# Attention and feed-forward on one core: the first feed-forward unit of a turn is issued ahead of the scores of the last key group

## The chip, the cores and the metric

The kernel runs on one core of a Trainium2 chip. The metric is the device time of one execution, in microseconds (us); lower is better. PE is TensorE (matmuls; PEld its weight loads), DVE is VectorE, ACT is ScalarE, POOL is GpSimd, and SP is SyncE, whose queue issues most transfers.

## The reference

Cosine attention for 8 batches of 12 heads (448 tokens, head size 64), then a feed-forward layer on the joined heads:

```python
q_n = q / (np.linalg.norm(q, axis=-1, keepdims=True) + 1e-06)
k_n = k / (np.linalg.norm(k, axis=-1, keepdims=True) + 1e-06)
scores = np.matmul(q_n, k_n.transpose(0, 1, 3, 2)) / tau
attn = np.exp(scores - np.max(scores, axis=-1, keepdims=True))
attn = attn / (np.sum(attn, axis=-1, keepdims=True) + 1e-09)
x = np.matmul(attn, v)          # heads joined: 3584 x 768
h = x @ w_in                    # 768 x 2048
g = h * np.clip(h + 3.0, 0.0, 6.0) / 6.0
out = g @ w_out                 # 2048 x 768
```

## The kernel before, in words

The work is cut into 48 pairs of heads (6 pairs to a batch), numbered i. For a pair, normalised q and k are held transposed with the head size on the partitions. The keys of a pair fall into four groups (`GROUPS`, line 364): groups 0 to 2 are 128 keys of each of the two heads (two matmuls each), and group 3, "M", is the last 64 keys of both heads together (one matmul). The steps of a pair are functions, each called by a short name through `do` (line 653):

- `SC`, `scores` (line 367): the score matmuls of one group, one PSUM bank for each matmul (L394). Groups 0 to 2 read `kz`, group 3 reads `km` from pair 14 on.
- `EX`, `exps` (line 400): exp on ACT from each bank to `at` (L412), which frees the bank.
- `VA`, `values` (line 425): 8 matmuls of a group that accumulate attn times v into the PSUM tile `PV` (L434).
- `FI`, `finish_values` (line 445): reciprocal and product on DVE, giving `on` (L454, L455).
- `XB` and `XP` (lines 482 and 493): a DMA on SP that transposes `on` of one pair or of two pairs into `xT` (L486, L498), the input of the feed-forward layer.

The keys and queries ahead are prepared by `LQ` (load, L174, on SP), `SQ` (square on POOL, L203), `RE` (reduce on DVE, L215), `NO` (four short activations on ACT, L231 to L234), `NM` (normalise on POOL, L246), `XD` (a transposing DMA on SP into `tT`, L302), `CK` (copy of keys from `tT` to `kz` on DVE, L341) and `CS` (copy of the last group's keys from `tT` to `km` on POOL, L351, once for two pairs, in odd turns). `LV` loads v and `VC` casts it on POOL (L186, L265).

The feed-forward layer is a stream of units. A first-layer unit (`mm1_unit`, line 508) is 6 matmuls into one bank (L514), then a relu on ACT (L523) and a product on DVE (L529), which writes `gT`. A second-layer unit (`mm2_unit`, line 541) is 16 matmuls of 384 columns (L550), a copy on ACT or DVE in turn (L561, L563), and two stores on SP (L571). A batch's first-layer units need `xT` of its six pairs. `whole_units(n)` (`UU`, line 639) issues n units, each with its work on ACT, DVE and SP.

Scores of groups and units of both kinds take PSUM banks from one ring of six (`next_bank`, line 136; `ring`, line 630), always the next one. A bank is taken again only when its reader has read it: the exp for scores, relu and product for a first-layer unit, the copy for a second-layer unit.

The schedule is written out by hand: every engine runs its instructions in the order in which the program issues them, and semaphores are put in between where one step needs another. Pairs 0 to 17 follow a list (`PLAN`). From pair 18 on (`FIRST`, line 18) each pair is one turn of the loop at line 700. In such a turn the program issues the last value step of the pair before that is still due for group 3, the scores of groups 0 to 2 (six matmuls, which take six banks in a row), their six exps, the value steps of groups 1 and 2 of the pair before, `FI` of that pair, and then the stretch that the change touches: group 3's scores and exp, the transposes on SP, one unit, the preparation of later pairs, and the remaining units (three or four a turn in all). The turn ends with the value step of group 0 of its own pair. After pair 47 the rest of the stream follows.

Of the kernel before, what the change touches and what calls it, by code (L numbers as in the profile page):

```python
# [61 lines left out]
def kernel(  # L62
# [590 lines left out]
    def do(op, *args):  # L653
        OPS[op](*args)
        key = (op,) + tuple(a for a in args if isinstance(a, int))
        if op not in ("RE", "NM", "LQ"):
            issued.add(key[:3] if op == "SC" else key)
# [27 lines left out]
    SC = [psum_s.tile([128, 2, 512], FP32, name=f"SC{n}", tag=f"SC{n}") for n in range(2)]  # L685
# [14 lines left out]
    for i in range(FIRST, NP):  # L700
        n_u = len(units[i])
        even = i % 2 == 0

        def prepare(*what):
            for op, n, *args in what:
                if n < (NP // 2 if op in ("NO", "LV") else NP):
                    do(op, n, *args)

        if i > FIRST:
            do("VA", i - 1, 3)  # L710
        for g in range(3):
            do("SC", i, g)
        for g in range(3):
            do("EX", i, g)
        for g in range(1, 4):
            if ("VA", i - 1, g) not in issued:
                do("VA", i - 1, g)
        do("FI", i - 1)
        do("SC", i, 3)
        do("EX", i, 3)  # L720

        if (i - 1) % HP > 3:
            do("XB", i - 1)
        elif even:
            do("XP", i - 2)
        if even:
            prepare(("XD", i + 2))
        do("UU", 1)
        if not even:
            prepare(("CS", i + 1))  # L730
        prepare(("SQ", i + 5, "p", 0, 7))
        n = 2
        do("UU", n - 1)
        if not even:
            prepare(("CK", i + 1), ("CK", i + 2))
        if not even:
            prepare(("NO", (i + 3) // 2))
        do("UU", n_u - n)
        prepare(("NM", i + 3, "p"), ("VC", i + 2, "p"), ("RE", i + 5))
        if even:  # L740
            prepare(("XD", i + 3))
        prepare(("LQ", i + 7))
        if not even:
            prepare(("LV", (i + 5) // 2))
        do("VA", i, 0)
# [42 lines left out]
```

## Time and profile before

| | us |
|---|---|
| median of three runs | 421.07 |
| lowest and highest of them | 419.57, 422.46 |
| the profiled execution, its time | 420.79 |
| the profiled execution, its span | 418.7 |

The span runs from the first to the last instruction on the engines; the 2.1 us beside it lie around the program. In the profile, L514 and the like are lines of the kernel; a tile's buffer number is left out, so the four banks M0 to M3 of the ring are all "M", and the other two are "Y" and "Z". The length of a matmul in the timeline (0.35 us for 448 columns) overlaps with that of the next, which starts before it ends; the spacing of the starts shows how fast PE goes. A square bracket behind a row gives the idle time of its engine before it and what ended it.

The loop's first turn, 18, begins on PE at 114.97 us; turn 19 at 124.65, turn 22 at 149.33, and the last, 47, at 347.90. A turn takes 6.75 to 9.7 us. The granted clock of TensorE was 1.00.

### The profile page before, as it was taken

The page shows a single profiled execution, that of the slowest core. Times are in us where ns is not written, and L with a number is a line of the kernel's source. Part 1 is how long each engine was busy: PE and PEld are TensorE (multiplying, and loading weights), DVE is VectorE, ACT ScalarE, POOL GpSimd, SP SyncE. Part 2 cuts the span into 40 slices and gives each one's busy share as a digit, 9 for nine tenths or more (in the row PEclk, how much of TensorE's full clock was granted, in tenths as well). Part 3 has the DMA queues.
Part 4 walks back from the last instruction along what each step waited for, and adds up shares of the span by engine and source line. Part 5 has one row for each costly group of instructions (what it writes and reads, how often), then busy time and mean ns, then how long its engine had stood idle before and what let it go on. Part 6 is the DMA issues. An engine that isn't in the chain of part 4 may idle for free.

```text
span 418.7 us, 9613 instructions
## 1 busy us (share of the span) xinstructions
PE 411.0 (98%) x3792; PEld 242.1 (58%) x3792; DVE 214.5 (51%) x419; ACT 268.3 (64%) x591; POOL 183.8 (44%) x190
## 2 busy tenths in 40 slices
PE   7999999999999999999999999999999999999996
PEld 5666556556655555555555555555555555655564
DVE  6898677855445445465445453555454343315410
ACT  6899998885557755857756775776765674105400
POOL 7899646454235466355375365374372300000000
PEclk9999999999999999999999999999999999999999
DMA  8999999789797866767986958777865431330033
GB/s 292 298 245 253 179 279 229 152 138 205 163 182 193 187 168 152 175 176 139 183 196 126 201 136 181 177 155 154 182 165 76 87 66 34 69 77 20 2 75 75
DMA packets 91564, 65.31 MB, mean 156 GB/s; under 512 B 56064, under 2 KB 89984, under 8 KB 91520
## 3 DMA queue, kind: packets, MB, share of 16 engines
q1 hardware_dynamic: 87728, 58.37, 61.2%
q0 software_dynamic: 3712, 6.29, 8.7%
q8 instruction: 29, 0.48, 0.5%
q14 instruction: 15, 0.12, 0.1%
q10 hardware_dynamic: 80, 0.05, 0.1%
HBM read 47.19 MB, written 11.01 MB: 139 GB/s over the span
## 4 chain that ended last, share of the span: by engine, by line
PE 97%; DVE 1%; DMA 1%; issue 0%; ACT 0%; ACTq 0%
PE M L514 24%; PE M L550 23%; PE PV L434 12%; PE Z L550 7%; PE Y L514 6%; PE Y L550 6%; PE Z L514 6%; PE M L394 5%; PE PV L621 3%; PE Y L394 1%; PE Z L394 1%; PE SC L394 1%; DMA xT<-on 1%; PE Z L291 1%; PE Y L616 1%; PE SC L391 0%
## 5 line engine op out<-in xcount | busy, mean ns | idle before, releaser
L550 PEld LDWEIGHTS <-gT 128*128 128x128 bf16 x912 | 88.6, 98 | 58.4
L412 ACT ACTIVATE at<-M 128x448 bf16<-128x448 f32 x199 | 96.8, 565 | 33.4 <-PE M L394 21.1
L514 PEld LDWEIGHTS <-w_in_sb 128*128 128x128 bf16 x768 | 73.3, 97 | 68.7 <-issue 8.2
L514 PE MATMUL M<-xT,w_in_sb 128*128 128x448 bf16 x522 | 107.2, 352 | 0.8 <-DMA xT<-on 0.8
L550 PE MATMUL M<-w_out_sb,gT 128*128 128x384 bf16 (+1 forms) x592 | 99.3, 324 | 0.0
L246 POOL TENSOR_TENSOR nrm<-raw,r 128x896 bf16<-128x896 f32 (+1 forms) x48 | 77.8, 1626 | 38.3 <-ACT r L234 28.6
L529 DVE SCALAR_TENSOR_TENSOR gT<-u,M 128x448 bf16<-128x448 bf16 x87 | 52.8, 619 | 56.5 <-ACT u L523 56.3
L203 POOL TENSOR_TENSOR sq<-raw 128x896 f32<-128x896 f32 (+3 forms) x39 | 63.5, 1629 | 13.3 <-DMA raw<-in_q_dram 6.3
L434 PEld LDWEIGHTS <-at 128*128 128x128 bf16 (+1 forms) x1536 | 54.8, 97 | 24.6 <-issue 15.4
L523 ACT ACTIVATE u<-M,bias 128x448 bf16<-128x448 f32 x87 | 55.3, 659 | 15.6 <-PE M L514 15.5
L434 PE MATMUL PV<-vx,at 128*128 128x65 bf16 (+1 forms) x1536 | 64.3, 194 | 0.2 <-DVE on L455 0.2
L215 DVE TENSOR_REDUCE n<-sq 128x14 f32<-128x896 f32 (+1 forms) x50 | 51.8, 1041 | 5.9 <-ACT sq L201 5.7
L351 POOL COPY km<-tT 64x128 bf16<-64x128 bf16 x34 | 9.9, 292 | 97.8 <-DMA tT<-nrm 65.2
L412 ACT ACTIVATE at<-Z 128x448 bf16<-128x448 f32 x48 | 27.0, 563 | 12.3 <-PE M L394 12.2
L455 DVE TENSOR_TENSOR on<-PV,rc 128x512 bf16<-128x512 f32 x48 | 33.2, 692 | 1.7
L563 DVE COPY o<-M 128x384 f32<-128x384 f32 x18 | 10.0, 558 | 46.6 <-PE M L550 38.6
L561 ACT COPY o<-M 128x384 f32<-128x384 f32 (+1 forms) x19 | 8.9, 471 | 38.5 <-PE M L550 37.6
L394 PE MATMUL M<-tT,kz 64*128 64x448 bf16 (+1 forms) x175 | 31.3, 351 | 0.0
L550 PE MATMUL Z<-w_out_sb,gT 128*128 128x384 bf16 (+1 forms) x176 | 29.1, 319 | 0.0
L265 POOL CAST vx<-vr 128x512 bf16<-128x512 f32 x44 | 27.6, 630 | 1.3 <-DMA vr<-in_v_dram 1.2
L412 ACT ACTIVATE at<-Y 128x448 bf16<-128x448 f32 x47 | 26.6, 567 | 2.2 <-PE Z L394 2.2
L514 PE MATMUL Y<-xT,w_in_sb 128*128 128x448 bf16 x126 | 27.3, 352 | 0.0
(78 smaller groups left out, 336.8 us busy)
## 6 DMA issues: line engine op xcount, KB each, us to landing
vr<-in_v_dram SPq DMA_DIRECT2D x96, 128.0 KB, 4.1
raw<-in_k_dram SPq DMA_DIRECT2D x24, 448.0 KB, 4.4
raw<-in_q_dram SPq DMA_DIRECT2D x24, 448.0 KB, 4.1
out_dram<-o SPq DMA_DIRECT2D x110, 96.0 KB, 2.2
w_in_sb<-in_moe_w_in_dram POOLq DMA_DIRECT2D x4, 768.0 KB, 11.1
w_out_sb<-in_moe_w_out_dram POOLq DMA_DIRECT2D x4, 768.0 KB, 9.3
tT<-nrm SPq DMA_TRANSPOSE x34, 3.4
xT<-on SPq DMA_TRANSPOSE x25, 4.0
```

The costliest lines, as they stand in the source:

```text
L203: engines[e].tensor_tensor(out=o, in0=i, in1=i, op=ALU.mult)
L215: nc.vector.tensor_reduce(out=n2s[d % 2][:, j % 2, c], in_=sq[:, :, :, :].rearrange("p g c d -> p (g c) d")[:, c, :], axis=AX.X, op=ALU.add,)
L246: engines[e].tensor_tensor(out=nrm[:, :, g, :].rearrange("p c g d -> p g c d"), in0=raw_of[j][:, g, :, :], in1=rs[d % 2][3][:, j % 2, :] . ...
L265: (engines[e].copy if e == "a" else engines[e].tensor_copy)(out=o, in_=f)
L394: nc.tensor.matmul(o, ks, qt[rows], start=True, stop=True)
L412: nc.scalar.activation(out=o, in_=x, func=AF.Exp, scale=inv_tau)
L434: nc.tensor.matmul(pv_out(j, h), at[rows, n, q_cols(i // HP, j)], vt[rows, 3 + h if name == "M" else 5 * h + int(name[1]), :], start=(name ...
L455: nc.vector.tensor_tensor(out=on[:, :, :, :].rearrange("p j h d -> p h j d"), in0=pv4[:, :, :, 0:D], in1=rc[:, :, :].to_broadcast([128, 2, ...
L514: nc.tensor.matmul(ps[:, 0:S], w_in_sb[:, cc, fc * 128 : (fc + 1) * 128], x[:, cc, 0:S], start=(cc == 0), stop=(cc == CC - 1),)
L523: nc.scalar.activation(out=u[:, :], in_=ps[:, 0:S], func=AF.Relu, bias=half_bias, scale=1.0 / 6.0)
L529: nc.vector.scalar_tensor_tensor(out=g[:, fc, c0 : c0 + S], in0=u[:, :], scalar=1.0, in1=ps[:, 0:S], op0=ALU.min, op1=ALU.mult,)
L550: nc.tensor.matmul(ps[:, 0:width], lhs, w_out_sb[:, fc, cols], start=(fc == 0), stop=(fc == FCN - 1),)
```

## The change

Group 3's scores and its exp are issued behind the turn's first unit, and so behind the transposes on SP that stand ahead of that unit, in turns 18 to 47. Nothing else is altered.

```diff
             if ("VA", i - 1, g) not in issued:
                 do("VA", i - 1, g)
         do("FI", i - 1)
-        do("SC", i, 3)
-        do("EX", i, 3)
 
         if (i - 1) % HP > 3:
             do("XB", i - 1)
...
         if even:
             prepare(("XD", i + 2))
         do("UU", 1)
+        do("SC", i, 3)
+        do("EX", i, 3)
         if not even:
             prepare(("CS", i + 1))
         prepare(("SQ", i + 5, "p", 0, 7))
```

As banks are handed out in the order of issue, the first unit now takes the bank that group 3's scores took, and the reverse. On PE the six matmuls of the unit come ahead of the one matmul of group 3; on ACT the unit's relu comes ahead of group 3's exp. The order of work on DVE, POOL and SP is that of before, apart from the names of the banks.

## The prediction

> **What bounds the kernel now.** I read the page first (busy shares, slices, chain), then the list of PE's waits in the stretch the change touches (124 to 352 us: turns 19 to 47), then the timeline of single turns around the moved step.
>
> ```profile
> span 418.7 us, 9613 instructions
> ...
> PE 411.0 (98%) x3792; PEld 242.1 (58%) x3792; DVE 214.5 (51%) x419; ACT 268.3 (64%) x591; POOL 183.8 (44%) x190
> ...
> PE   7999999999999999999999999999999999999996
> ...
> PE 97%; DVE 1%; DMA 1%; issue 0%; ACT 0%; ACTq 0%
> ```
>
> PE is at 9 in every slice but the first and the last and carries 97% of the chain that ended last; the granted clock is 1.00 throughout. A busy PE need not be at its peak, so I looked at start-to-start times: a projection group of 16 matmuls takes 2.60 us (162.5 ns for 384 columns), a first-layer unit of 6 takes 1.13 us (189 ns for 448 columns), the same in every turn. So only what makes PE stand still can be won, and the wait list shows one such place:
>
> ```profile
> PE M L514 <- DMA xT<-on: 0.8, 1, 0.8
> ```
>
> That list misses gaps hidden under the modelled length of a matmul (0.35 us shown against 0.19 between starts). The timeline of turn 22, whose scores begin at 149.33, shows one (start us, length us, engine, line, operation):
>
> ```profile
> 149.33 0.35 PE L394 MATMUL Y<-tT,kz 64*128 64x448 bf16 x1
> ...
> 149.72 0.54 ACT L412 ACTIVATE at<-Y 128x448 bf16<-128x448 f32 x1 [0.18 <-PE Z L394]
> ...
> 149.99 0.66 PE L434 MATMUL PV<-vx,at 128*128 128x65 bf16 x16
> 150.16 0.54 ACT L412 ACTIVATE at<-Z 128x448 bf16<-128x448 f32 x1
> 150.46 0.10 PEld L394 LDWEIGHTS <-km 128*128 128x128 bf16 x1
> 150.49 0.35 PE L394 MATMUL Y<-tT,km 128*128 128x448 bf16 x1
> ...
> 150.74 1.29 PE L514 MATMUL Z<-xT,w_in_sb 128*128 128x448 bf16 x6
> ...
> 152.28 0.60 ACT L412 ACTIVATE at<-Y 128x448 bf16<-128x448 f32 x1
> 152.70 0.69 ACT L523 ACTIVATE u<-Z,bias 128x448 bf16<-128x448 f32 x1
> ```
>
> The six score matmuls fill all six banks of the ring; the last group (L394 with km) takes the first bank again (Y), the first unit the second (Z). The exp that empties Z ends at 150.70, and the unit starts at 150.74, 0.25 us after the km matmul instead of 0.19. The starts in ns say the same for all 29 turns 19 to 47: km to unit is 250 to 255 ns, the unit starts 1.415 us after the turn's first score matmul each time, and the exp of the second bank ends at 1.364 or 1.365. Where that exp had ended long before, the step is 188 to 190 ns; turn 18, with 24 value matmuls instead of 16 ahead of it, is such a place:
>
> ```profile
> 116.52 0.35 PE L394 MATMUL M<-tT,km 128*128 128x448 bf16 x1
> ...
> 116.71 1.30 PE L514 MATMUL M<-xT,w_in_sb 128*128 128x448 bf16 x6
> ```
>
> So there is a wait of 0.065 us (0.254 less 0.189) in each of 29 turns, 1.9 us in all, plus the 0.84 us for xT, which stands in turn 19:
>
> ```profile
> 124.17 1.22 SPq L486 DMA_TRANSPOSE xT<-on  x1
> ...
> 125.81 0.35 PE L394 MATMUL M<-tT,km 128*128 128x448 bf16 x1
> 126.07 1.11 PE L514 MATMUL M<-xT,w_in_sb 128*128 128x448 bf16 x5
> ...
> 128.02 1.49 PE L514 MATMUL M<-xT,w_in_sb 128*128 128x448 bf16 x7 [0.84 <-DMA xT<-on]
> 128.87 0.64 POOL L351 COPY km<-tT 64x128 bf16<-64x128 bf16 x2 [6.68 <-DMA tT<-nrm]
> ```
>
> **The change, step by step.** Per turn it moves one weight load and one matmul on PE and one exp on ACT, behind one unit. That unit is first-layer in each of turns 18 to 47 (L514 after every km matmul): 6 matmuls on PE, one relu on ACT, one product on DVE, no DMA. Instruction counts are unchanged. DVE and POOL keep their order of work, and so does SP: the xT and tT transposes stand ahead of the unit and the stores behind it both before and after.
>
> *The bank wait.* The unit now takes the first bank and the km matmul the second. The unit could start where the km matmul did, 1.160 to 1.165 us into the turn; its bank's exp ends at 0.930, plus the 0.05 us seen from exp end to start, 0.98. No wait, with 0.18 us to spare. The km matmul comes 1.13 us later, at about 2.29, and its exp ended at 1.365: no wait. The second unit stands at the same place as before less 0.065; its bank's exp ends at 1.80, it starts near 2.48. Gain: 0.065 x 28 turns (20 to 47) = 1.82 us. Turn 18 had no such wait and gains nothing.
>
> The Trainium skill (Perfetto Trace Analysis, Optimization Strategy) reads a gap that repeats on the saturated engine as a possible sign of too few buffers. By that rule a reorder over the same six banks would win nothing and only the xT loss below would remain, about 421.3; the row that shows the first bank free 0.18 us early decides against it.
>
> *Turn 19.* The unit's sixth matmul waits for the xT transpose, which lands at 127.98 by its semaphore. It sits on SP behind a load at 123.48, in an order that does not change, and starts from work of turn 18. So the sixth matmul still starts at 128.02. Before, the km matmul ran under cover of that wait; now it follows, and the second unit starts 0.19 us later than before (128.40 for 128.21). Loss: 0.19 us; the bank wait of this turn is worth nothing, as it lay ahead of the xT wait.
>
> *xT at later batch starts.* Turns 25, 31, 37 and 43 take a new batch's xT in the first unit, which now starts 0.254 us earlier. In turn 25 the landing is at 174.69 and the sixth matmul at 174.74 + 0.94 = 175.68; after, with the 0.14 us that turns 20 to 24 win net of the 0.19, it is at about 175.29: 0.6 us to spare. Turn 37: landing 270.10, sixth 271.03, 0.68 to spare if its SP queue, fed by stores of the turns just before, moves along with PE. Turns 31 and 43 have 2.7 us or more. Cost: nothing.
>
> *The exp on ACT.* It follows the relu, which needs the unit done (2.45 us into the turn); the sixth exp ends at 3.11 anyway, so ACT has no hole and the two only change places: relu about 0.5 us earlier, exp until about 4.2 instead of 3.55. Its reader is the value step at the turn's end, 6.3 us in, even in the shortest turn (6.75 us). Cost nothing; without that cover, at most the 0.6 us of one exp a turn.
>
> *km on POOL.* This is the wait the move sharpens. In odd turns POOL's two km copies wait for tT and for the km matmul, which reads the old km. In turn 31 the km matmul starts at 222.16 and the copy at 222.58, 0.42 us later. After, the copy can't start before 1.16 + 1.13 + 0.42 = 2.71 us into the turn. It now starts at 1.84 (turn 23), 2.31 (25), 1.58 (31), 2.22 (33), 2.40 (35), 2.32 (37), 1.63 (39), 1.58 (43 and 45), and later than 2.71 in the rest: 0.3 to 1.1 us late in nine turns, 6.9 us together. Queued behind it on POOL are square, normalise and the V cast; the reduce on DVE that reads the square starts 2.1 to 5.3 us after the square ends in the turns with a delay; the normalise mostly waits 0.4 to 2.0 us for ACT's norms anyway; km itself is read over 5 us later; and POOL idles 5 to 7 us ahead of each km copy. Cost: nothing. Bounds: 0, as there is no way to gain, and 6.9 if all of it reached PE; I take 0, by those slacks.
>
> **Sum.** -1.82 + 0.19 = -1.63 us. The profiled execution took 420.79 with a span of 418.7, so 417.1 and about 419.2; it lies 0.28 under the median of the three runs (421.07), from which the prediction is **419.4**.
>
> **The rivals.**
> 1. *The 0.065 us is no wait but a turnaround that stays.* For it: PE's wait list doesn't show it. Against: it is absent in turn 18, and the sum of the steps before it is constant to 1 ns while they themselves vary by 5, as for a wait on another engine. Only the loss of turn 19 remains: 421.07 + 0.19 = 421.3.
> 2. *An xT wait returns.* The L486 transposes land 1.2 to 4.2 us after SP has issued them; those of turns 25 and 37 took 2.0 and 2.1. Were both to take 4.2, each would be 1.5 us past its margin: 419.4 + 3.0 = 422.4. Against: traffic around them is the same.
> 3. *Slower: POOL becomes the bound through km.* Place: the km copies of nine odd turns. It decides when a delay of 1.1 us eats the smallest slack behind it, 2.1 us at the reduce of turn 33, which then holds DVE's reciprocal and bank releases. Price at most 6.9: 419.4 + 6.9 = 426.3. Against: turn 33 is delayed by 0.5 only.
>
> **How the numbers follow.** Forecast 0.80, rival 1 0.10, rival 2 0.05, rival 3 0.03, something faster still 0.02. The three runs of before span 419.57 to 422.46, so a median of a few runs may stray by some 0.8 to 1.5. Low: all 29 waits without the loss of turn 19 (-1.9) less 1.3, 417.9. High: rival 1 and 0.3 of stray, 421.6. About 1% (4.2 us) is what a measurement of this kernel can tell from no change: faster by over that needs more than twice all of PE's gaps that the bank wait makes, 0.03; slower needs rival 3 or both xT waits and more, 0.04; within, 0.93.
>
> **What would show it.** Right: in turns 20 to 47 the value matmuls are followed directly by L514, six starts of 0.19, then km, then the next unit 0.19 later, with no 0.25 step; the turn's length falls from 7.89 to 7.82 (turn 21 and its like); turn 19 still waits for xT, now about 1.1 us; km copies start no earlier than 2.7 us into odd turns; the span is near 417.1. Wrong: a 0.25 step that reappears elsewhere in the turn, a second xT row in PE's waits, or DVE's reduce starting on POOL's square in odd turns.

## The result, and the profile after

| | before | after |
|---|---|---|
| median of 22 runs, us | 419.74 | 418.01 |
| lowest and highest, us | 419.37, 423.16 | 417.61, 420.42 |
| span of the profiled execution, us | 418.7 | 415.9 |

After to before is 0.9947, with a 95% interval of 0.9930 to 0.9964. The medians lie 1.73 us apart. The time lies at the low edge of the predicted range (417.9 to 421.6): over 22 runs, before stands at 419.74 and not at the 421.07 from which the prediction subtracted.

The page of after, in three of the lines that were shown of before:

```profile
span 415.9 us, 9613 instructions
...
PE 409.2 (98%) x3792; PEld 242.4 (58%) x3792; DVE 217.0 (52%) x419; ACT 268.0 (64%) x591; POOL 183.1 (44%) x190
...
PE 98%; DVE 1%; issue 0%; ACT 0%; ACTq 0%
```

The bound is the same, and the 1% of DMA has gone from the chain. With it went the row for xT from the list of PE's waits; over the whole program the list now holds two waits only, both in its first 30 us. Turn 22 of after, in the timeline (start us, length us, engine, line, operation):

```profile
148.27 0.35 PE L394 MATMUL Y<-tT,kz 64*128 64x448 bf16 x1
...
148.66 0.54 ACT L412 ACTIVATE at<-Y 128x448 bf16<-128x448 f32 x1 [0.18 <-PE Z L394]
...
148.94 0.66 PE L434 MATMUL PV<-vx,at 128*128 128x65 bf16 x16
149.10 0.54 ACT L412 ACTIVATE at<-Z 128x448 bf16<-128x448 f32 x1
...
149.44 1.30 PE L514 MATMUL Y<-xT,w_in_sb 128*128 128x448 bf16 x6
...
150.57 0.35 PE L394 MATMUL Z<-tT,km 128*128 128x448 bf16 x1
...
150.76 1.11 PE L514 MATMUL M<-xT,w_in_sb 128*128 128x448 bf16 x5
151.22 0.68 ACT L523 ACTIVATE u<-Y,bias 128x448 bf16<-128x448 f32 x1
```

The unit takes bank Y, which the first exp left at 149.20, and starts at 149.44, straight behind the value matmuls. km takes Z, free since 149.64, at 150.57; the next unit follows 0.19 us later. The 0.25 us step is gone. The turn's length falls from 7.89 to about 7.83 us, and the long and short turns shrink alike (9.35 to 9.29, 6.75 to 6.69). From the start of turn 20 to that of turn 47, 27 turns, before took 214.35 us and after 212.64: 1.71 us, or 0.063 a turn.

Turn 19 is where the two profiled executions differ by more than the predicted amount:

```profile
122.23 1.21 SPq L486 DMA_TRANSPOSE xT<-on  x1
...
125.95 1.30 PE L514 MATMUL M<-xT,w_in_sb 128*128 128x448 bf16 x6
127.09 0.35 PE L394 MATMUL M<-tT,km 128*128 128x448 bf16 x1
127.28 1.30 PE L514 MATMUL M<-xT,w_in_sb 128*128 128x448 bf16 x6
```

SP issued the transposing DMA at 122.23 where it had been 124.17; it landed at 126.06, and all six matmuls of the unit run without a stop. The turn took 7.83 us against 8.90. Of these 1.07 us, 0.065 are the bank wait and 1.00 the wait for xT (the wait list gave it as 0.84, since it counts from the modelled end of the fifth matmul). The spans differ by 2.74 us: 1.71 + 1.07, some 0.1 from the start of turn 47 to the end, less 0.14 by which turn 18 began later.

On POOL, turn 31 after:

```profile
222.09 0.64 POOL L351 COPY km<-tT 64x128 bf16<-64x128 bf16 x2 [6.91 <-PE M L394]
222.81 1.68 POOL L203 TENSOR_TENSOR sq<-raw 128x896 f32<-128x896 f32 x1
225.08 1.69 POOL L246 TENSOR_TENSOR nrm<-raw,r 128x896 bf16<-128x896 f32 x1 [0.59 <-ACT r L234]
226.10 1.08 DVE L215 TENSOR_REDUCE n<-sq 128x14 f32<-128x896 f32 x1
```

The copy starts 2.71 us into the turn (which begins at 219.38), as worked out, 1.13 later than before. What ends its wait is now PE's km matmul. The normalise still waits for ACT (0.59 us where it was 1.72), and the reduce starts 1.6 us after the square has ended: the delay ends in the slack.

### The profile page after: what moved, and what is told of

Same layout as the page of the kernel before. It is cut to its first block, busy times and chain, and to the rows that moved or that the text cites. A ratio compares the mean times of both kernels' runs of the same rounds, so it can differ in the third digit from the quotient of the medians.

```text
span 415.9 us, 9613 instructions
## 1 busy us (share of the span) xinstructions
PE 409.2 (98%) x3792; PEld 242.4 (58%) x3792; DVE 217.0 (52%) x419; ACT 268.0 (64%) x591; POOL 183.1 (44%) x190
## 4 chain that ended last, share of the span: by engine, by line
PE 98%; DVE 1%; issue 0%; ACT 0%; ACTq 0%
PE M L514 24%; PE M L550 23%; PE PV L434 12%; PE Z L550 7%; PE Y L514 6%; PE Y L550 6%; PE M L394 6%; PE Z L514 5%; PE PV L621 3%; PE Z L394 1%; PE Y L394 1%; PE SC L394 1%; PE Z L291 1%; PE Y L616 1%; PE SC L391 0%; DVE on L455 0%
## 5 line engine op out<-in xcount | busy, mean ns | idle before, releaser
L412 ACT ACTIVATE at<-M 128x448 bf16<-128x448 f32 x198 | 98.6, 565 | 33.2 <-PE M L394 21.0
L514 PE MATMUL M<-xT,w_in_sb 128*128 128x448 bf16 x528 | 110.7, 352 | 0.0
L514 PEld LDWEIGHTS <-w_in_sb 128*128 128x128 bf16 x768 | 71.6, 98 | 62.9 <-issue 2.5
L529 DVE SCALAR_TENSOR_TENSOR gT<-u,M 128x448 bf16<-128x448 bf16 x88 | 54.6, 620 | 54.3 <-ACT u L523 54.0
L523 ACT ACTIVATE u<-M,bias 128x448 bf16<-128x448 f32 x88 | 58.1, 661 | 14.4 <-PE M L514 14.3
```

Of the source, the lines that this page charges most:

```text
L412: nc.scalar.activation(out=o, in_=x, func=AF.Exp, scale=inv_tau)
L514: nc.tensor.matmul(ps[:, 0:S], w_in_sb[:, cc, fc * 128 : (fc + 1) * 128], x[:, cc, 0:S], start=(cc == 0), stop=(cc == CC - 1),)
L523: nc.scalar.activation(out=u[:, :], in_=ps[:, 0:S], func=AF.Relu, bias=half_bias, scale=1.0 / 6.0)
L529: nc.vector.scalar_tensor_tensor(out=g[:, fc, c0 : c0 + S], in0=u[:, :], scalar=1.0, in1=ps[:, 0:S], op0=ALU.min, op1=ALU.mult,)
```

## The experiments

**Order and banks, one at a time.** The change exchanges two things at once for PE: the order and the banks. Two kernels alter one of them each. The first keeps the order of before and exchanges the banks, from turn 18 on:

```diff
         do("FI", i - 1)
+        ring_n[0] += 1
         do("SC", i, 3)
+        ring_n[0] -= 2
         do("EX", i, 3)
...
         do("UU", 1)
+        ring_n[0] += 1
```

> The order of issue is that of before (group 3's scores, then the first unit); only the two PSUM banks are exchanged, so that group 3's scores take the ring's second bank and the unit the first. Theory (the step of 0.254 us is a wait for the exp of the second bank, which ends 1.365 us into the turn): now the km matmul waits for it, starts at 1.415 instead of 1.160 and the unit 0.19 later, at 1.60 instead of 1.415. Every turn from 19 on is 0.19 us longer, 7.89 becomes 8.08, 29 turns make 5.5 us: ratio to before about 1.013. Rival (the step is a turnaround between group 3's scores and a unit, whatever the banks): the starts stay at 1.160 and 1.415, ratio 1.000.

The ratio to before was 1.0146 (1.0096 to 1.0196), the median 426.99 us. Its span of 426.2 also holds a late start: turn 18, the first that the edit touches, began 3.07 us later than in before. The trace shows why: PE waited 2.08 us for POOL at the start of the program, and the 3.41 us from 13.22 on, where PE was busy throughout, had half the granted clock (0.50):

```profile
12.67 0.56 PE L291 MATMUL Z<-ident,nrm 128*128 128x128 bf16 x7 [2.08 <-POOL nrm L246]
```

Two of the four runs, this one among them, had a mean clock of 0.996 and took 428.35 and 428.57 us; the two at 1.00 took 425.64 and 425.47. So the turns are the better measure: 8.08 us each where they were 7.89, as worked out. Turn 22 begins at 151.97:

```profile
152.79 0.54 ACT L412 ACTIVATE at<-Z 128x448 bf16<-128x448 f32 x1
...
153.38 0.35 PE L394 MATMUL Z<-tT,km 128*128 128x448 bf16 x1
153.57 1.29 PE L514 MATMUL Y<-xT,w_in_sb 128*128 128x448 bf16 x6
```

The exp that empties Z ends at 153.33, and km starts 0.05 us later, 1.42 into the turn; the unit follows at 0.19. So the wait goes where bank Z goes, and the step from km to a unit is 0.19 in itself.

The second kernel has the order of after and the banks of before:

```diff
+        ring_n[0] += 1
         do("UU", 1)
+        ring_n[0] -= 2
         do("SC", i, 3)
+        ring_n[0] += 1
         do("EX", i, 3)
```

> The order of issue is that of after (first unit, then group 3's scores), but each keeps the bank that it had before: the unit the second, group 3's scores the first. Theory (bank wait): the unit waits for the second bank's exp and starts at 1.415 us into the turn as before, km follows at 2.55 and the second unit at 2.74, against 2.55 before: 0.19 us longer a turn, 5.5 us in all, ratio to before about 1.013, so the whole gain turns into a loss. Rival (the gain comes from the order alone, with the value matmuls followed by a unit): the gain of after stays, ratio 0.995.

The ratio was 1.0102 (1.0067 to 1.0137), the median 425.17 us, and the turns took 8.08 us; turn 22 begins at 148.69:

```profile
149.52 0.54 ACT L412 ACTIVATE at<-Z 128x448 bf16<-128x448 f32 x1
...
150.11 1.29 PE L514 MATMUL Z<-xT,w_in_sb 128*128 128x448 bf16 x6
151.24 0.35 PE L394 MATMUL Y<-tT,km 128*128 128x448 bf16 x1
```

The unit waits for the end of that exp (150.06) and starts 1.42 into the turn. The order alone thus gains nothing and loses 0.19 us a turn; only order and banks together, so that whichever step comes first takes the bank that is free first, remove the wait. The rivals of a turnaround and of a gain by order alone both fall.

**The order on ACT alone.** The unit's matmuls, then group 3's scores and exp, then the unit's relu:

```diff
-        do("UU", 1)
+        unit()
         do("SC", i, 3)
         do("EX", i, 3)
+        for e in "av":
+            while post[e]:
+                finish_units(e)
```

> PE's order is that of after; on ACT the exp of group 3 is put ahead of the first unit's relu again. Theory (the gain is PE's bank wait alone): as after, ratio to before 0.995 to 0.996, turns of 7.82 us; the relu and its product come about 0.5 us later and nobody waits for them. Rival (the earlier relu is worth something): part of the gain goes, turns above 7.82 us.

The ratio was 0.9946 (0.9920 to 0.9972), the median 418.02 us, the span 415.9; the 27 turns from 20 on take 212.64 us, to the hundredth what they take in after. In turn 22 the relu starts 3.37 us into the turn instead of 2.95, and the turns on PE keep their length. The earlier relu is worth nothing.

**Group 3's scores behind two units.**

```diff
         do("UU", 1)
+        n = 2
+        do("UU", n - 1)
         do("SC", i, 3)
         do("EX", i, 3)
...
-        n = 2
-        do("UU", n - 1)
```

> Group 3's scores, their exp and the copies of km behind them are moved on, behind the turn's second unit. Theory (one unit ahead already removes the whole wait, and POOL has slack): turns stay at 7.82 us, ratio as after, 0.995 to 0.996, although km copies in odd turns can't start before 3.8 us into the turn where the second unit is of the first layer, 5.3 where it is of the second. Rival (POOL becomes the bound through km): the squares end after DVE is ready for the reduce in some odd turns, and these turns get longer by up to 1 us each; ratio above 0.997.

The ratio was 0.9938 (0.9909 to 0.9967), the median 418.15 us, the span 415.6, and the 27 turns again took 212.64 us. Turn 33, with the smallest slack by the prediction, begins at 234.69:

```profile
238.12 0.35 PE L394 MATMUL Z<-tT,km 128*128 128x448 bf16 x1
...
238.54 0.64 POOL L351 COPY km<-tT 64x128 bf16<-64x128 bf16 x2 [7.21 <-PE Z L394]
239.26 1.68 POOL L203 TENSOR_TENSOR sq<-raw 128x896 f32<-128x896 f32 x1
...
241.58 1.08 DVE L215 TENSOR_REDUCE n<-sq 128x14 f32<-128x896 f32 x1
```

The copy starts 3.85 us in, and the reduce 0.64 after the square has ended. Even twice the delay of the change stays inside POOL's slack; whether a third unit would use up the rest was not tried.

**The wait for xT in turn 19: more executions of both kernels.** The kernel before, unaltered, was profiled three more times, and after twice more:

> The kernel before once more, for the wait of 0.84 us for xT in turn 19. Theory (it is chance, set by how far SP lags before turn 18): SP issues the transposing DMA at another time than 124.17 us, and the wait is shorter, absent or longer; without it the span is near 417.5. Rival (it belongs to the kernel before): 0.7 to 1.1 us again.

> A second look at the kernel before, with the same expectations: by chance, the wait in turn 19 differs from look to look; if it belongs to the kernel, it is 0.7 to 1.1 us in both.

> A third look at the kernel before for the xT wait in turn 19. Chance: turn 19 is 7.89 us where the DMA lands less than 2.3 us into the turn, longer where it lands later. All other turns as in the other two looks.

> A second look at the kernel after. The bank wait is gone in all turns: turns of 7.82 us, 27 turns from 20 on take 212.6 us against 214.35 before. Chance in turn 19: 7.83 us where xT lands less than 2.1 us into the turn, and 0.19 us more than the delay alone where it lands later.

> A third look at the kernel after, with the same expectations as the second.

The landing of xT, counted from the start of turn 19, by its semaphore; the unit's sixth matmul is due at 2.36 in before and 2.11 in after:

| execution | landing | turn 19 | turns 20 to 46 | time |
|---|---|---|---|---|
| before, the profile of the prediction | 3.32 | 8.90 | 214.35 | 420.79 |
| before, three more executions | 0.79, 1.31, 1.01 | 7.89 each | 214.35, 214.35, 214.37 | 419.47, 419.93, 421.15 |
| after, first execution | 1.27 | 7.83 | 212.64 | 418.05 |
| after, two more executions | 0.71, 1.10 | 7.83 each | 212.64 each | 417.74, 417.76 |

Turn 19 in the first of the three more executions of before:

```profile
121.26 1.21 SPq L486 DMA_TRANSPOSE xT<-on  x1
...
125.54 0.35 PE L394 MATMUL M<-tT,km 128*128 128x448 bf16 x1
125.80 2.43 PE L514 MATMUL M<-xT,w_in_sb 128*128 128x448 bf16 x12
```

No wait for xT stands there, and the 0.26 from km to the unit does. So the wait was there once in four executions of before, and its absence in after is nothing that the change has to explain. The times agree: the median of 22 runs of before, 419.74, lies among executions without the wait (419.47, 419.93) and not at the 420.79 of the one with it. (The execution of 421.15 us has no such wait; its turn 18 began 1.4 us late, at 116.33, which lies ahead of all that the change touches.) SP was late ahead of turn 19 in that one execution; what made it late was not followed further and stays open.

**The same wait, forced.** To see what the move costs where the wait is present, the transposing DMA of pair 17 is put behind the units of turn 18, in both kernels:

```diff
-        if (i - 1) % HP > 3:
+        if i == FIRST:
+            pass
+        elif (i - 1) % HP > 3:
             do("XB", i - 1)
...
         do("UU", n_u - n)
+        if i == FIRST:
+            do("XB", i - 1)
```

> The kernel before, with the transposing DMA of pair 17's values (xT) issued behind all units of turn 18 instead of ahead of them, so that turn 19 must wait for it. The DMA lands at about 130 us, and the first unit's sixth matmul waits about 3 us. It gives the length of turn 19 with a sure wait and group 3's scores ahead of the unit, to be set beside the same edit of the kernel after.

> The same late transposing DMA in the kernel after. Theory of the prediction (where the xT wait is present, the move costs one km matmul, as group 3's scores no longer run under the wait): from the landing of xT to the end of turn 19 it takes 0.19 us more than in the same edit of the kernel before, and turns 20 on are 7.82 against 7.89 us; all in all 1.6 us faster than that kernel. Rival (the move also makes the wait itself shorter or longer): the time from the start of turn 19 to the landing differs by more than SP's own variation explains.

The kernel before, edited so, took 421.39 us (ratio to before 1.0033, 1.0002 to 1.0064), and after, edited so, 420.42 (1.0018, 0.9982 to 1.0054). The wait was shorter than the expected 3 us: 1.66 in the one and 2.48 in the other. xT landed 3.98 and 4.54 us into turn 19; these lie 0.57 apart, about as far as the landings of the unedited kernels without a wait (0.71 to 1.31), so one execution of each can't tell whether the move alters the wait itself. In before the two units follow each other across the wait, with km long done:

```profile
128.39 1.49 PE L514 MATMUL M<-xT,w_in_sb 128*128 128x448 bf16 x7 [1.50 <-DMA xT<-on]
```

In after the sixth matmul is followed by km, then the next unit:

```profile
129.14 0.35 PE L514 MATMUL M<-xT,w_in_sb 128*128 128x448 bf16 x1 [2.32 <-DMA xT<-on]
129.33 0.35 PE L394 MATMUL M<-tT,km 128*128 128x448 bf16 x1
129.52 1.72 PE L514 MATMUL M<-xT,w_in_sb 128*128 128x448 bf16 x6
```

From the sixth matmul to the start of turn 20 it takes 5.53 us in all executions of before, with the wait and without, and 5.72 in all executions of after that have no wait: 0.19 us of km behind instead of ahead, as predicted. In the forced execution of after it took 7.40. The 0.19 of km stands in the rows above; the rest has another reason, the clock: the windows view (span, then busy time and count of PE, PEld, DVE, ACT and POOL, then clock, DMA share, GB/s) for the same stretch of the edited before and, below, the edited after:

```profile
130.20:133.80 3.60, 3.60 (x31) 2.16 (x29) 2.75 (x5) 1.97 (x7) 2.08 (x2) 1.00 0.34 116
```

```profile
130.20:133.80 3.60, 3.60 (x13) 1.47 (x11) 1.76 (x4) 2.21 (x7) 2.58 (x3) 0.53 0.44 123
```

The granted clock was half for 3.41 us, from 130.26 on, behind the wait of 2.48 us, which cost about 1.7 (7.40 less 5.72). The expected 1.6 us between the two kernels was not met (0.97 between the medians). The clock is not all of the reason: only three of the ten runs of the edited after had a mean clock of 0.996 or less, and the other seven spread from 419.52 to 422.19, while eight of the ten of the edited before lie between 421.16 and 421.57. So these times are no clean measure of the 0.19; the spacing alone shows it.

**xT earlier.** After, with that DMA ahead of a load on SP:

```diff
-    if FIRST + 6 < NP:
-        do("LQ", FIRST + 6)
...
             do("XP", i - 2)
+        if i == FIRST:
+            do("LQ", FIRST + 6)
```

> The kernel after, with the transposing DMA of pair 17's values (xT for turn 19) issued on SP ahead of the load of raw tile 24 instead of behind it. Theory (in most executions turn 19 doesn't wait for xT): SP issues it about 0.65 us earlier, turn 19 is 7.83 us as in the profile of after, and the median is that of after, ratio to before 0.995 to 0.996. Rival (the wait in turn 19 is there in most timed executions): up to 0.65 us faster than after, ratio 0.993 to 0.994.

The kernel took 418.06 us, ratio to before 0.9961 (0.9936 to 0.9986); xT landed 1.44 us ahead of the start of turn 19, SP having issued it 0.8 to 1.4 us earlier against that start than in the three executions of after (about 0.65 was expected). The time is that of after: where nothing waits for xT, there is nothing to win. No version tried is faster than after by more than the runs can tell.

## Why the prediction was right or wrong

The mechanism of the gain was predicted rightly. What failed is the term of turn 19, the base that the sum starts from, and the bound for what can be told from no change.

- *PE is the bound, and only its stops can be won:* right. The number of instructions and their spacing are the same, and the turns got shorter by the stops alone.
- *A bank wait of 0.065 us in 29 turns:* right in place and mechanism, as the two kernels with banks or order alone show; 0.063 us a turn measured. Its size over 28 turns was put at 1.82 us; 27 turns gave 1.71, with turn 47 about 1.8.
- *Turn 19, a loss of 0.19 us:* this step failed. The prediction put it that xT "lands at 127.98 by its semaphore", "in an order that does not change", so that "the sixth matmul still starts at 128.02". The order did not change, but the time did: one execution was taken for the kernel. In three further executions of before, and in every execution of after and of the variants that left the DMA in place, xT landed 0.8 to 1.8 us before it was needed. Turn 19 therefore gains its 0.065 like the others (7.89 to 7.83 us), and the sum becomes about -1.9 by the predicted size instead of -1.63. The price itself (0.19 us where the wait is present) was right, as the spacing shows.
- *The level:* this failed too. 419.4 was taken from a median of three runs, 421.07, which lay 1.33 us above that of 22 (419.74). That is nearly all of the 1.39 us to 418.01: the same -1.63 from 419.74 gives 418.11. The 0.10 us left is less than the 0.25 by which the term of turn 19 was off, and too small for these medians to tell. The predicted difference of 1.63 us, 0.9961 of 421.07, lies inside the measured interval, near its upper end. That 418.01 lies in the range at all is owed to the 1.3 us that its low end allows for a stray of the base.
- *What can be told from no change:* put at 1% (4.2 us), which was too wide. Over 22 runs of each the interval came out at 0.17% to either side, so that a gain of 0.5% is clear of zero. The chances put 0.93 on "within", next to a forecast of a gain; a bound of that width could not tell the gain from none.
- *The exp on ACT, cost nothing:* right; with ACT's order put back, the 27 turns take the same time to the hundredth. The exp ends 4.07 us into the turn, 4.2 forecast.
- *km on POOL, cost nothing:* right. The copy starts at 2.71 us as worked out, and DVE's reduce never waited for it, nor with twice the delay.
- *xT at later batch starts, cost nothing:* right; no second xT wait appeared.

The Trainium skill's reading of a repeating gap as a possible sign of too few buffers (Perfetto Trace Analysis, Optimization Strategy), set against the row in the prediction, was a good place to look but the wrong remedy here: the same six banks serve without a wait once the first taker gets the first free.

## What to carry to other kernels

Where steps take buffers in rotation, a short step ahead of a long one needs two buffers almost at once (here 0.19 us apart); with the long one first, the second buffer has the whole of that time (here 1.13 us) to come free. Compare start-to-start times with the spacing of the same instruction elsewhere: the list of waits counts from the modelled end of a matmul, so that it hid the 0.065 us and gave 0.84 for 1.00. And a wait for a DMA should be seen in several executions before it becomes a term of a sum; the same holds for the time that the sum starts from.

## What the runs showed of the hardware

A stop of 2.48 us between two matmuls was followed by 3.41 us at half the granted clock, and cost about 1.7 us more; in that stretch the starts of 448-column matmuls lie 0.37 us apart instead of 0.19. The start of the kernel with the banks alone exchanged shows it a second time, behind a stop of 2.08 us. A stop of 1.66 us was not followed by it, and neither was the 1.00 us in the profile of before. In the 3.41 us ahead of the two drops PE was busy for 1.11 and 1.33 us; in the 3.41 us that hold nearly all of the stop of 1.66 us, for 1.92. The Trainium skill (TensorE: Matmul & The Clock Gate, Part 1: The HAM clock gate) gives an idle window of about 3.4 us before the clock is halved; the half-clock stretches here had that length, but a shorter stop was enough to bring each on.

One stretch of 3.41 us at half clock takes the mean clock of an execution of 420 us to 0.996. Of the 52 further runs of before whose clocks are on record, eight had a mean of 0.996 or less, and they are the eight longest, 422.44 to 424.20 us; none of the others took more than 421.73. These runs left no trace, so where in the program their clock fell is not shown. It does show why a median of three can lie high: one of the three runs of before that the prediction started from, at 422.46, lies among such times, though its own clock is not on record.
